# Moving a block's input scaling, its cast, a query cast and the output scaling to GpSimd, with a new order of steps

## The chip, the cores and the metric

The kernel runs on one core of one Trainium2 chip. The metric is the device time of the whole kernel in microseconds, as the median of several runs. Four engines compute: TensorE (PE in the profile, its weight loads PEld), VectorE (DVE), ScalarE (ACT) and GpSimd (POOL); SyncE (SP) issues most DMAs. Each engine takes its instructions strictly in program order and waits on semaphores for the others.

## The reference

An attention over pooled keys is followed by two feed-forward layers of 128 x 2048 x 128, all on 12288 rows of 128 columns:

```python
def _attn_ref(q, kv, w_sr):                # kv is pooled 4 x 4 to 768 keys; k = v = pooled @ w_sr
    s = scale * (q @ k.transpose(0, 2, 1))
    s = s - s.max(-1, keepdims=True)
    a = np.exp(s)
    a /= a.sum(-1, keepdims=True) + 1e-09
    return (a @ v).astype(np.float32)

def _moe_ref(x, w_in, w_out):              # layer 1
    h = x @ w_in
    relu6 = np.clip(h + 3.0, 0.0, 6.0)
    g = h * relu6 / 6.0
    return (g @ w_out).astype(np.float32)

def _moe2_ref(x, w_in, w_out):             # layer 2, beta = 1
    h = x @ w_in
    g = np.where(h >= beta, h, np.where(h <= -beta, 0.0, (h + beta) ** 2 / (4.0 * beta)))
    return (g @ w_out).astype(np.float32)
```

## The kernel before

The rows are cut into 24 blocks of 512, the 2048 hidden columns into 8 pairs of two chunks of 128. One block and one pair make a slot's work for a layer: slot T works on pair T of layer 1 (192 pairs in all) and on pair T - 11 of layer 2. Nearly every operand is kept as two fp16 parts, a high part (a cast) and a low part (what the cast lost), and each product is three matmuls: high x high, low x high, high x low. So a slot has 12 matmuls into the hidden activations (line 707, tiles `h`, a ring of four buffers in PSUM) and 12 into the two accumulators (line 725, `acc`), all of 512 columns. In a block of eight slots, four slots (even ones) also have the six score matmuls of 128 queries (line 593), and two (1 and 5 mod 8) the 18 matmuls that multiply weights by values (line 673).

The order of all steps is written out by hand: a prologue, then for slots below 22 the string RAMP, from slot 22 on the string SLOT. A name followed by `:n` serves slot T - n when slot T is issued. Every step issues to fixed engines, so a string is at once the order of five queues. The names, with the line of their main instruction and 0 and 1 for the two chunks:

- Layer 1: `a` matmuls (707, TensorE), `r` rectifier (749, ScalarE), `m` product (756, VectorE), `c` cast to the high part (785, ScalarE), `l` low part (791, GpSimd), `o` output matmuls (725).
- Layer 2: `A` matmuls (707), `K` clip (764, VectorE), `Q` square (772, ScalarE), `X` maximum (777, VectorE, it frees the `h` buffer), `C` cast (785, ScalarE), `L` low part (791, GpSimd), `O` output matmuls (725).
- Between the layers, once per block: `D` maximum of layer 1's output (490, VectorE), `R` copy of it to `xr` (496, ScalarE), `P` its sum over partitions (499, TensorE), `F` the scale and five columns of constants made from it (506 to 511, VectorE), `G` the high part x2h (516, ScalarE), `H` the low part x2l (521, VectorE). With `:1` and `:2` these fall in slots 1 and 2 mod 8; layer 2 reads x2 from slot 3 mod 8 on.
- Output, once per block: `T` transpose of the accumulator (734, VectorE), `U` scaling (739, ScalarE) and four DMAs (741, SyncE), in slot 5 mod 8.
- Queries, once per block: `q` transpose (558, VectorE) and a load, `i` high part (565, ScalarE), `j` low part (571, GpSimd); `q` and `i` in slot 2 mod 8.
- Attention: `s` scores, `n` their maximum (604, VectorE), `e` exponential (633, ScalarE), `t` sum and reciprocal (642, 645, VectorE), `u` high part of the weights (652, ScalarE), `w` low part (657, VectorE) and a transposing DMA (663), `v` values (673), `z` and `y` the two parts of layer 1's input (681 ScalarE, 687 VectorE).
- `B0` to `B2` convert weights; they are over by slot 22, and so is `x`.

Of the kernel before, what the change touches and what calls it, by code (L numbers as in the profile page):

```python
# [15 lines left out]
ACTF = mybir.ActivationFunctionType  # L16
ALU = mybir.AluOpType
# [20 lines left out]
RAMP = """a0:0 r0:0 a1:0 r1:0 t:1 u:1 m0:0 m1:0 D:1 R:1 G:2 H:2 x:0 A0:0 K0:0 A1:0 K1:0 C0:1 L0:1 C1:1 L1:1 c0:0 l0:0 c1:0 l1:0  # L38
T:3 U:3 Q0:0 Q1:0 s:0 n:0 w:1 P:1 F:1 X0:0 X1:0 e:0 v:0 z:0 y:0 q:0 i:0 j:0 B1:1 B2:2 B0:0 f o:1 O:2"""
SLOT = """  # L40
a0 r0 B2:3 o:2 a1 l1:1 u:1 O:3 G:2 r1 y:1 D:1 B0:2 C0:1 R:1 m0 A0 A1 v w:1 c0 H:2 C1:1 j:1 m1 c1 K0
K1 Q0 P:1 T:3 L0:1 s n q F:1 Q1 B1:3 L1:1 X0 e X1 f:1 t U:3 i z l0
"""
MX = ((0, "m8"), (1, "m10 m12"), (2, "m14 a2 b2"), (3, "s2 m9"), (4, "m11 m13"), (5, "m15 a3 b3"), (6, "s3 bk"))

# [14 lines left out]
def tile_attn_moe_moe2(  # L60
# [15 lines left out]
    nc = tc.nc  # L76
# [7 lines left out]
    KC = NKEY // 128  # L84
    scale = 1.0 / float(C) ** 0.5
# [32 lines left out]
    b_k = const.tile([128, 5], FP32, name="b_k")  # L118
# [12 lines left out]
    def new_h():  # L131
        return ps_h.tile([128, 512], FP32, tag="h", name="h")


    did = set()

    def step(name, key, *before):
        for n in before:
            assert (n, key) in did, (name, key, n)
        did.add((name, key))  # L140
# [27 lines left out]
    def died(rec):  # L168
        clock[0] += 1
        rec["dead"] = clock[0]  # L170
# [25 lines left out]
    def w_max(job):  # L196
        m, which, i = job
        n = 2 * m + (which == "out")
        nc.vector.tensor_reduce(out=mw[n][:, i:i + 1], in_=wst[job][0][:, :, 1].bitcast(FP32),
                                axis=AX.X, op=ALU.max, apply_absolute_value=True)  # L200

    def w_top(n):
        nc.vector.tensor_reduce(out=mw[n][:, 0:1], in_=mw[n], axis=AX.X, op=ALU.max)

    def w_top_pool(n):
# [2 lines left out]
        w_tops[n] = mw[n][:, 1:2]  # L210

    def w_top_row(n):
        step("row", n)
        w_tops[n] = new_h()
        nc.tensor.transpose(w_tops[n][0:1, 0:128], mw[n][:, 0:1], ident)

# [151 lines left out]
    def pool_ps(m):  # L368
        if m not in ps_pool:
            ps_pool[m] = new_h()  # L370
        return ps_pool[m]

    def kv_pool(i):
        m, mode = i // 2, KV_MODE[i]
        t = kv_t[i][0]
        if mode == "V":
            nc.vector.tensor_tensor(out=t[:, :, 0:2], in0=t[:, :, 0:2], in1=t[:, :, 2:4], op=ALU.add)
            nc.vector.tensor_tensor(out=t[:, :, 0], in0=t[:, :, 0], in1=t[:, :, 1], op=ALU.add)
            return
        ps = pool_ps(m)  # L380
        for g in range(2):
            p0 = (2 * (i % 2) + g) * 32
            for j in range(4):
                if mode == "P":
                    nc.tensor.matmul(ps[p0:p0 + 32, :128], pool_m, t[:, g, j], start=(j == 0), stop=(j == 3))
                else:
                    nc.tensor.matmul(
                        ps[:, 128 + p0:160 + p0], t[:, g, j], pool_m, start=(j == 0), stop=(j == 3)
                    )
        died(kv_t[i][1])  # L390
        if mode == "P" and i % 2 == 1:
            nc.scalar.copy(out=pk[:, m * 128:(m + 1) * 128], in_=ps[:, :128])

    def kv_sum_mm(i):
        t, rec = kv_t[i]
        ps = pool_ps(i // 2)
        for g in range(2):
            c0 = 128 + (2 * (i % 2) + g) * 32
            nc.tensor.matmul(ps[:, c0:c0 + 32], t[:, g, 0], pool_m)
        died(rec)  # L400
# [20 lines left out]

    def v_max(m):
        vp = vps[m // 3][:, (m % 3) * 128:(m % 3 + 1) * 128]
        nc.vector.tensor_reduce(
            out=mx[:, m:m + 1], in_=vp, axis=AX.X, op=ALU.max, apply_absolute_value=True
        )

    def v_scale():
        nc.vector.tensor_reduce(out=mx[:, 0:1], in_=mx, axis=AX.X, op=ALU.max)
        nc.tensor.transpose(vps[0][0:1, 384:512], mx[:, 0:1], ident)  # L430

# [54 lines left out]
    bs_t, mb_t, xr_t, x2_ps = {}, {}, {}, {}  # L486
# [15 lines left out]
    def x2_scales(b):  # L502
        step("F", b, "P")
        assert ("bk", 0) in did
        t = bs_t[b]
        nc.vector.tensor_scalar(out=t[:, 2:3], in0=x2_ps.pop(b)[:, 0:1], scalar1=2.0 ** -40, scalar2=None, op0=ALU.max)  # L506
        nc.vector.tensor_scalar(out=t.bitcast(U32)[:, 3:4], in0=t.bitcast(U32)[:, 2:3], scalar1=0x7F800000,
                                scalar2=None, op0=ALU.bitwise_and)
        nc.vector.reciprocal(out=t[:, 4:5], in_=t[:, 3:4])
        nc.vector.tensor_scalar(out=t[:, 5:8], in0=b_k[:, 0:3], scalar1=t[:, 4:5], scalar2=None, op0=ALU.mult)  # L510
        nc.vector.tensor_scalar(out=t[:, 8:10], in0=b_k[:, 3:5], scalar1=t[:, 3:4], scalar2=None, op0=ALU.mult)  # L511

    def x2_hi(b):
        step("G", b, "F")
        x2_t[b] = [x_p.tile([128, BLK], FP16, tag=f"x2{p}", name=f"x2{p}") for p in "hl"]
        nc.scalar.activation(out=x2_t[b][0], in_=xr_t[b], func=ACTF.Copy, scale=bs_t[b][:, 5:6])

    def x2_lo(b):
        step("H", b, "G")
        hi, lo = x2_t[b]  # L520
        nc.vector.scalar_tensor_tensor(  # L521
            out=lo, in0=xr_t.pop(b), scalar=bs_t[b][:, 5:6], in1=hi, op0=ALU.mult, op1=ALU.subtract
        )

    def v_hi(sv):
        for h in range(2):
# [15 lines left out]
    q_t, qT_t, e_t, at_t, x_t, x2_t, o_t = {}, {}, {}, {}, {}, {}, {}  # L542
# [19 lines left out]

    def q_hi(b):
        hi, lo, t = qT_t[b]
        nc.scalar.copy(out=hi, in_=t)
        step("i", b)

    def q_lo(b):
# [167 lines left out]

    def o_scale(b):
        o = o_t.pop(b)
        nc.scalar.activation(out=o, in_=o, func=ACTF.Copy, scale=bs_t[b][:, 9:10])
        for a in range(4):  # L740
            nc.sync.dma_start(
                out=o_v[b, a], in_=o[32 * a:32 * a + 32].rearrange("i (b j) -> i b j", j=32)
            )
# [51 lines left out]
    def ok(s):  # L795
        return 0 <= s < NS

    steps_m1 = {f"m{n}": (lambda n=n: w_max(w_jobs[n])) for n in range(8, 16)}
    for n in (2, 3):
        steps_m1 |= {f"a{n}": lambda n=n: (w_top(n), w_top_row(n)), f"b{n}": lambda n=n: w_top_all(n),  # L800
                     f"s{n}": lambda n=n: w_scale8(n)}
# [97 lines left out]
    with tc.manual_schedule():  # L899
# [6 lines left out]
            out=pool_m.rearrange("p (a q) -> p a q", a=4),  # L906
            in_=ident.rearrange("p (a r q) -> p a q r", a=4, r=4), axis=AX.X, op=ALU.add,
# [16 lines left out]
        for n, v in enumerate((2.0 ** -5, 2.0 ** -2, 2.0 ** -30)):  # L924
            nc.vector.memset(w_k[:, n:n + 1], v)

        steps = {f"k{i}": (lambda i=i: kv_pool(i)) for i in range(NG // 2)}
        steps |= {f"g{i}": (lambda i=i: kv_sum_mm(i)) for i in range(NG // 2)}
        for m in range(KC):
# [7 lines left out]
        for n in range(8):  # L937
            steps[f"m{n}"] = lambda n=n: w_max(w_jobs[n])
        steps |= {"ia": lambda: (w_top(0), w_top_pool(0)), "ib": lambda: (w_scales(0), w_unit(0)),
                  "oa": lambda: w_top(1), "ot": lambda: w_top_row(1), "ob": lambda: w_top_all(1),  # L940
                  "oc": lambda: w_scale8(1)}
        for j in range(4):
# [47 lines left out]
```

## Time and profile before

| What | Value |
|---|---|
| runs | 1339.81, 1341.2, 1343.64 us; median 1341.2 |
| profiled execution | 1342.52 us, its span 1340.7 us |
| TensorE busy | 1247.0 us, 93% |
| VectorE busy | 1187.5 us, 89% |
| ScalarE busy | 1158.6 us, 86% |
| GpSimd busy | 941.9 us, 70% |
| mean granted TensorE clock | 0.978 of full speed |

The profile shows one execution. Its span runs from the first to the last instruction, and 1.8 us of the execution's time lie outside. Times in rows are microseconds from the span's start; `L521` is line 521 of the kernel; `x2` at the end of a row counts merged instructions; what stands in square brackets is the engine's idle time before the row, with what ended it. A wait for several semaphores is put down to the one that came last. The ends of matmuls are modelled, so their starts are the better guide.

### The profile page before, as it was taken

The numbers are of one execution on the slowest core, as the hardware profiler recorded it, in microseconds if no ns is written. First come the engines' busy times: TensorE is split into PE (matmuls) and PEld (weight loads), VectorE is DVE, ScalarE is ACT, GpSimd is POOL, SyncE is SP. The second block draws the span as 40 slices with busy tenths as digits, with TensorE's granted clock in tenths as the row PEclk, the third lists the DMA queues.
The fourth block names the chain that finished last, engine by engine and source line by source line (L and its number), as shares of the span: only waits on it lengthen the run. The fifth ranks groups of instructions, "written<-read, shape, count | busy, mean of one in ns | idle before, by whom it ended". The sixth has DMA issues, their size and how long they took to land.

```text
span 1340.7 us, 19138 instructions
## 1 busy us (share of the span) xinstructions
PE 1247.0 (93%) x6280; PEld 662.2 (49%) x6280; DVE 1187.5 (89%) x1944; ACT 1158.6 (86%) x2028; POOL 941.9 (70%) x825
## 2 busy tenths in 40 slices
PE   7466789999999999999999999999999999999996
PEld 6333445455455555555455555555555555555442
DVE  4676799999999999999999999999999999999887
ACT  3465788998999998999998998899999999999986
POOL 2244687777777777777777777777777777777874
PEclk9687899999999999999999999999999999999998
DMA  8821113222222212222122122222122121121000
GB/s 301 219 44 36 32 26 50 44 39 45 39 37 53 40 35 52 36 40 52 32 44 52 33 44 49 33 46 47 36 45 44 37 48 36 32 45 32 1 9 17
DMA packets 260788, 66.32 MB, mean 49 GB/s; under 512 B 252368, under 2 KB 256592, under 8 KB 260688
## 3 DMA queue, kind: packets, MB, share of 16 engines
q1 hardware_dynamic: 257888, 63.73, 23.8%
q10 hardware_dynamic: 2800, 1.38, 0.4%
q8 instruction: 49, 0.80, 0.2%
q14 instruction: 51, 0.42, 0.1%
HBM read 21.04 MB, written 6.29 MB: 20 GB/s over the span
## 4 chain that ended last, share of the span: by engine, by line
PE 59%; DVE 20%; ACT 11%; issue 1%; DVEq 0%; ACTq 0%
PE h L707 24%; PE acc L725 23%; PE s L673 6%; PE s L593 5%; DVE g L777 5%; ACT h L785 4%; DVE g L764 3%; ACT t L749 2%; DVE t L756 2%; DVE x2l L521 2%; DVE bs L511 2%; ACT g L772 2%; ACT a L652 2%; DVE nm L604 2%; DVE bs L510 1%
## 5 line engine op out<-in xcount | busy, mean ns | idle before, releaser
L791 POOL TENSOR_TENSOR l<-g,h 128x512 f16<-128x512 f32 x382 | 450.1, 1196 | 274.7 <-DVE a L657 135.0
L791 POOL TENSOR_TENSOR l<-t,h 128x512 f16<-128x512 f32 x382 | 438.6, 1170 | 42.2 <-ACT h L785 39.2
L764 DVE TENSOR_SCALAR g<-h,bs 128x512 f32<-128x512 f32 x384 | 292.7, 804 | 23.7 <-PE h L707 23.6
L756 DVE SCALAR_TENSOR_TENSOR t<-t,h 128x512 f32<-128x512 f32 x384 | 255.8, 682 | 29.1 <-ACT t L749 25.9
L777 DVE SCALAR_TENSOR_TENSOR g<-g,bs,h 128x512 f32<-128x512 f32 x384 | 267.9, 737 | 14.0 <-ACT g L772 13.2
L785 ACT CAST h<-g 128x512 f16<-128x512 f32 x384 | 235.1, 615 | 42.2 <-PE acc L725 40.2
L749 ACT ACTIVATE t<-h,h_sc 128x512 f32<-128x512 f32 x384 | 252.5, 676 | 21.1 <-PE h L707 21.0
L772 ACT ACTIVATE g<-g,bs 128x512 f32<-128x512 f32 x384 | 259.7, 717 | 6.8 <-DVE g L764 3.6
L785 ACT CAST h<-t 128x512 f16<-128x512 f32 x384 | 235.6, 618 | 22.6 <-DVE t L756 21.2
L707 PE MATMUL h<-x2h,wi1h 128*128 128x512 f16 x384 | 145.6, 379 | 16.8 <-DVE g L777 16.8
L707 PE MATMUL h<-xh,wi0h 128*128 128x512 f16 x384 | 146.8, 382 | 10.2 <-ACT xh L681 6.2
L725 PE MATMUL acc<-h,wo1h 128*128 128x512 f16 x384 | 146.0, 380 | 3.9 <-DVE o L734 3.8
L725 PE MATMUL acc<-l,wo1h 128*128 128x512 f16 x384 | 145.9, 380 | 1.5 <-POOL l L791 1.5
L725 PE MATMUL acc<-h,wo0h 128*128 128x512 f16 x384 | 146.5, 381 | 0.8 <-DVE bs L506 0.8
L725 PE MATMUL acc<-l,wo0h 128*128 128x512 f16 x384 | 146.3, 381 | 0.5 <-DVE l L791 0.5
L725 PE MATMUL acc<-h,wo0l 128*128 128x512 f16 x384 | 146.1, 380 | 0.0
L725 PE MATMUL acc<-h,wo1l 128*128 128x512 f16 x384 | 146.0, 380 | 0.0
L707 PE MATMUL h<-xl,wi0h 128*128 128x512 f16 x384 | 145.9, 380 | 0.1
L707 PE MATMUL h<-xh,wi0l 128*128 128x512 f16 x384 | 146.0, 380 | 0.0
L707 PE MATMUL h<-x2h,wi1l 128*128 128x512 f16 x384 | 145.7, 379 | 0.0
L707 PE MATMUL h<-x2l,wi1h 128*128 128x512 f16 x384 | 145.5, 379 | 0.0
L707 PEld LDWEIGHTS <-wi1h 128*128 128x128 f16 x768 | 75.1, 98 | 113.9 <-issue 26.9
(183 smaller groups left out, 1843.6 us busy)
## 6 DMA issues: line engine op xcount, KB each, us to landing
out_dram<-o SPq DMA_DIRECT2D x96, 64.0 KB, 1.9
q<-in_q_dram SPq DMA_DIRECT2D x92, 64.0 KB, 2.3
wst<-in_kv_dram SPq DMA_DIRECT2D x9, 512.0 KB, 7.5
wst<-in_moe_w_in_dram SPq DMA_DIRECT2D x6, 512.0 KB, 6.2
wst<-in_moe_w_out_dram SPq DMA_DIRECT2D x5, 512.0 KB, 4.8
at<-a SPq DMA_TRANSPOSE x96, 3.7
g<-in_moe_w_out_dram SPq DMA_DIRECT2D x2, 512.0 KB, 7.9
g<-in_moe_w_in_dram SPq DMA_DIRECT2D x1, 512.0 KB, 4.2
```

Of the source, the lines that this page charges most:

```text
L511: nc.vector.tensor_scalar(out=t[:, 8:10], in0=b_k[:, 3:5], scalar1=t[:, 3:4], scalar2=None, op0=ALU.mult)
L593: nc.tensor.matmul(ps[h], l[:, js], r[:, ks], start=(n == 0), stop=(n == 2))
L673: nc.tensor.matmul(ps, l[:, k, :], r[:, k, :], start=(n == 0), stop=(n == 3 * KC - 1))
L707: nc.tensor.matmul(ps, l[:, ws], r, start=(n == 0), stop=(n == 2))
L725: nc.tensor.matmul(acc[m], l[:, ws], r[:, k, :], start=(c == 0 and i == 0), stop=(c == NPAIR - 1 and i == 5))
L749: nc.scalar.activation(out=g_t[0, s][:, k], in_=h_t[0, s, k], func=ACTF.Relu, scale=h_sc, bias=0.5 * H_SC)
L756: nc.vector.scalar_tensor_tensor(out=g, in0=g, scalar=H_SC, in1=h_t.pop((0, s, k)), op0=ALU.min, op1=ALU.mult)
L764: nc.vector.tensor_scalar(out=g_t[1, s][:, k], in0=h_t[1, s, k], scalar1=bs_t[s // NPAIR][:, 6:7], scalar2=bs_t[s // NPAIR][:, 7:8], op0=A ...
L772: nc.scalar.activation(out=g, in_=g, func=ACTF.Square, scale=bs_t[s // NPAIR][:, 8:9], bias=0.5)
L777: nc.vector.scalar_tensor_tensor(out=g, in0=g, scalar=bs_t[s // NPAIR][:, 6:7], in1=h_t.pop((1, s, k)), op0=ALU.mult, op1=ALU.max)
L785: nc.scalar.copy(out=hl_t[m, s][0][:, k], in_=g_t[m, s][:, k])
L791: eng.tensor_tensor(out=lo[:, k], in0=g_t[m, s][:, k], in1=hi[:, k], op=ALU.subtract)
```

## The change

Five things change, and nothing else that issues an instruction:

- The two products that make the five columns of constants (510, 511) leave `F` on VectorE and become the first two instructions of `G` on GpSimd.
- `G` now scales `xr` in place on GpSimd, and `H` makes the high part by a cast and the low part by a subtraction, both on GpSimd. Before, ScalarE made the high part by a scaled copy, and VectorE the low part in one instruction that scaled and subtracted.
- `U` scales the output on GpSimd in place of ScalarE.
- `i` casts the queries on GpSimd in place of ScalarE, for blocks from 2 on.
- SLOT has a new order. RAMP stays, so in slots below 22 the moved steps keep their places.

```diff
 SLOT = """
-a0 r0 B2:3 o:2 a1 l1:1 u:1 O:3 G:2 r1 y:1 D:1 B0:2 C0:1 R:1 m0 A0 A1 v w:1 c0 H:2 C1:1 j:1 m1 c1 K0
-K1 Q0 P:1 T:3 L0:1 s n q F:1 Q1 B1:3 L1:1 X0 e X1 f:1 t U:3 i z l0
+a0 L1:2 X1:1 t:1 r0 u:1 l0:1 o:2 z:1 a1 D:1 O:3 r1 A0 A1 q l1:1 G:2 y:1 v m0 w:1 C0:1 m1 R:1 T:3 i
+C1:1 c0 K0 K1 P:1 f:1 s j:1 U:3 c1 Q0 n B0:2 Q1 F:1 L0:1 H:2 B2:2 X0 B1:4 e
 """
...
         nc.vector.reciprocal(out=t[:, 4:5], in_=t[:, 3:4])
-        nc.vector.tensor_scalar(out=t[:, 5:8], in0=b_k[:, 0:3], scalar1=t[:, 4:5], scalar2=None, op0=ALU.mult)
-        nc.vector.tensor_scalar(out=t[:, 8:10], in0=b_k[:, 3:5], scalar1=t[:, 3:4], scalar2=None, op0=ALU.mult)
 
     def x2_hi(b):
         step("G", b, "F")
+        t, xr = bs_t[b], xr_t[b]
         x2_t[b] = [x_p.tile([128, BLK], FP16, tag=f"x2{p}", name=f"x2{p}") for p in "hl"]
-        nc.scalar.activation(out=x2_t[b][0], in_=xr_t[b], func=ACTF.Copy, scale=bs_t[b][:, 5:6])
+        nc.gpsimd.tensor_scalar(out=t[:, 5:8], in0=b_k[:, 0:3], scalar1=t[:, 4:5], scalar2=None, op0=ALU.mult)
+        nc.gpsimd.tensor_scalar(out=t[:, 8:10], in0=b_k[:, 3:5], scalar1=t[:, 3:4], scalar2=None, op0=ALU.mult)
+        nc.gpsimd.tensor_scalar(out=xr, in0=xr, scalar1=t[:, 5:6], scalar2=None, op0=ALU.mult)
 
     def x2_lo(b):
         step("H", b, "G")
         hi, lo = x2_t[b]
-        nc.vector.scalar_tensor_tensor(
-            out=lo, in0=xr_t.pop(b), scalar=bs_t[b][:, 5:6], in1=hi, op0=ALU.mult, op1=ALU.subtract
-        )
+        xr = xr_t.pop(b)
+        nc.gpsimd.tensor_copy(out=hi, in_=xr)
+        nc.gpsimd.tensor_tensor(out=lo, in0=xr, in1=hi, op=ALU.subtract)
...
     def q_hi(b):
         hi, lo, t = qT_t[b]
-        nc.scalar.copy(out=hi, in_=t)
+        (nc.gpsimd.tensor_copy if b > 1 else nc.scalar.copy)(out=hi, in_=t)
         step("i", b)
...
     def o_scale(b):
         o = o_t.pop(b)
-        nc.scalar.activation(out=o, in_=o, func=ACTF.Copy, scale=bs_t[b][:, 9:10])
+        nc.gpsimd.tensor_scalar(out=o, in0=o, scalar1=bs_t[b][:, 9:10], scalar2=None, op0=ALU.mult)
```

The rest of the diff adds assertions on the order of steps, which issue nothing.

## Rows read from the trace of the kernel before

**Rows 1.** The chain that ended last, in time: start us, us, what.

```profile
248.69 1.97 PE s L673 x18
...
704.71 1.97 PE s L673 x18
...
755.83 1.97 PE s L673 x18
...
805.94 1.97 PE s L673 x18
...
1160.72 1.97 PE s L673 x18
```

**Rows 2.** The same chain, six matmuls of 512 columns and six of scores.

```profile
798.39 1.29 PE h L707 x6
799.68 1.06 PE s L593 x6
```

**Rows 3.** Timeline, line 521 and GpSimd in two neighbouring blocks: start, us, engine, line.

```profile
711.37 1.73 DVE L521 SCALAR_TENSOR_TENSOR x2l<-xr,bs,x2h 128x512 f16<-128x512 f32 x1
711.38 2.73 POOL L791 TENSOR_TENSOR l<-g,h 128x512 f16<-128x512 f32 x2 [2.20 <-ACT h L785]
...
762.47 0.74 DVE L521 SCALAR_TENSOR_TENSOR x2l<-xr,bs,x2h 128x512 f16<-128x512 f32 x1
762.50 2.86 POOL L791 TENSOR_TENSOR l<-g,h 128x512 f16<-128x512 f32 x2 [2.21 <-ACT h L785]
```

**Rows 4.** Four lines alone: ns minimum/median/maximum, first and last start us.

```profile
L510 DVE TENSOR_SCALAR bs<-b_k,bs x24: 478/764/942, 139.9 to 1299.7; 128x3 f32<-128x3 f32 x24
L511 DVE TENSOR_SCALAR bs<-b_k,bs x24: 215/1198/1203, 140.7 to 1300.1; 128x2 f32<-128x2 f32 x24
L521 DVE SCALAR_TENSOR_TENSOR x2l<-xr,bs,x2h x24: 736/744/1733, 148.1 to 1301.5; 128x512 f16<-128x512 f32 x24
L657 DVE SCALAR_TENSOR_TENSOR a<-e,rc,a x96: 999/1018/1839, 46.3 to 1223.8; 128x768 f16<-128x768 f32 x96
```

**Rows 5.** Timeline of slots 106 to 108, four engines.

```profile
758.02 2.27 POOL L791 TENSOR_TENSOR l<-t,h 128x512 f16<-128x512 f32 x2
...
761.74 0.62 ACT L785 CAST h<-g 128x512 f16<-128x512 f32 x1 [0.61 <-PE acc L725]
...
765.17 0.94 DVE L604 TENSOR_REDUCE nm<-s 128x1 f32<-128x768 f32 x1
...
766.66 1.36 DVE L777 SCALAR_TENSOR_TENSOR g<-g,bs,h 128x512 f32<-128x512 f32 x2
...
767.79 0.38 PE L707 MATMUL h<-x2h,wi1h 128*128 128x512 f16 x1
...
772.60 1.41 DVE L777 SCALAR_TENSOR_TENSOR g<-g,bs,h 128x512 f32<-128x512 f32 x2 [0.21 <-ACT g L772]
...
773.40 0.38 PE L707 MATMUL h<-x2h,wi1h 128*128 128x512 f16 x1 [0.27 <-DVE g L777]
```

**Rows 6.** Groups on GpSimd: xcount, busy us, mean ns of one, idle us before.

```profile
L791 POOL TENSOR_TENSOR l<-t,h 128x512 f16<-128x512 f32 x382 | 438.6, 1170 | 42.2 <-ACT h L785 39.2 <-DVE bs L507 3.0
L571 POOL TENSOR_TENSOR ql<-qT,qh 128x512 fp32r<-128x512 f32 x24 | 30.6, 1273 | 36.8 <-ACT qh L565 35.6
...
L333 POOL CAST wo1h<-wst 128x512 f16<-128x512 f32 x4 | 2.6, 649 | 0.0
```

**Rows 7.** Timeline, TensorE at the start of slot 12.

```profile
154.34 0.38 PE L707 MATMUL h<-xh,wi0h 128*128 128x512 f16 x1 [2.71 <-DVE t L756]
```

**Rows 8.** Timeline of the tail, VectorE and TensorE.

```profile
1311.12 1.52 DVE L764 TENSOR_SCALAR g<-h,bs 128x512 f32<-128x512 f32 x2
1312.56 0.71 DVE L734 STREAM_TRANSPOSE o<-acc 128x512 f32<-128x512 f32 x1
...
1313.32 0.61 PE L725 MATMUL acc<-h,wo1h 128*128 128x512 f16 x1 [3.79 <-DVE o L734]
1313.72 0.63 PE L725 MATMUL acc<-l,wo1h 128*128 128x512 f16 x1
```

More of the change, by code (lines that the diff above doesn't have):

```diff
@@ L198, in w_max @@
         n = 2 * m + (which == "out")
+        step("max", (n, i))
         nc.vector.tensor_reduce(out=mw[n][:, i:i + 1], in_=wst[job][0][:, :, 1].bitcast(FP32),
@@ L204, in w_top @@
     def w_top(n):
+        step("top", n)
+        for i in range(4):
+            assert ("max", (n, i)) in did
         nc.vector.tensor_reduce(out=mw[n][:, 0:1], in_=mw[n], axis=AX.X, op=ALU.max)
@@ L212, in w_top_row @@
     def w_top_row(n):
-        step("row", n)
+        step("row", n, "top")
         w_tops[n] = new_h()
@@ L374, in kv_pool @@
         m, mode = i // 2, KV_MODE[i]
+        step("k", i)
         t = kv_t[i][0]
@@ L395, in kv_sum_mm @@
         t, rec = kv_t[i]
+        step("g", i, "k")
         ps = pool_ps(i // 2)
@@ L423, in v_max @@
         vp = vps[m // 3][:, (m % 3) * 128:(m % 3 + 1) * 128]
+        step("y", m)
         nc.vector.tensor_reduce(
@@ L428, in v_scale @@
     def v_scale():
+        for m in range(KC):
+            assert ("y", m) in did
         nc.vector.tensor_reduce(out=mx[:, 0:1], in_=mx, axis=AX.X, op=ALU.max)
```

## The prediction

> **What bounds the kernel now.** I read the page's engine table first: TensorE is busy 93% of the span, VectorE 89%, ScalarE 86%, GpSimd 70%. A busy TensorE proves little, because the ends of matmuls are modelled, so I went on to the chain that ended last. In it the 18 matmuls that multiply attention weights by values come back twice in each block of eight slots, and two such pieces, eight slots apart, give the length of a block [rows 1]. There are only two lengths: 755.83 - 704.71 = 51.12 us, a long block, and 805.94 - 755.83 = 50.11 us, a short one. From 248.69 to 1160.72 there are 18 blocks in 912.03 us: 18 x 50.11 = 901.98, and the other 10.05 us make 10 long blocks and 8 short ones. One more short block follows.
>
> What would a block take if TensorE never waited? Six matmuls of 512 columns take 1.29 us, a group of six score matmuls 1.06 [rows 2], 18 value matmuls 1.97 [rows 1]. A slot has four groups of the first kind, a block four score groups and two value groups: 32 x 1.29 + 4 x 1.06 + 2 x 1.97 = 49.5 us. With the rounding of 1.29 (one matmul is some 0.2155 us) and the switches between kinds I take 49.7. So a long block holds 1.4 us of waiting and a short one 0.4: 10 x 1.4 + 9 x 0.4 = 17.6 us. TensorE bounds the middle of the kernel, and this is all that any change to the other engines can win there.
>
> Where does a long block's extra 1.0 us come from? From one instruction: VectorE's line 521 (layer 2's low part) takes 1.73 us in a long block and 0.74 in a short one [rows 3]. In the long one GpSimd's subtraction starts within 0.01 us of it, in the short one 0.03 us after it. Lines 510 and 511, which multiply three and two columns, show the same: from 0.48 to 0.94 us and from 0.215 to 1.20 us for almost no data, medians 0.76 and 1.20 [rows 4]. These instructions touch nothing but on-chip memory, and stand still while a GpSimd instruction runs. The delayed VectorE queue reaches TensorE through the ring of buffers for the hidden activations: even in the short block the first layer-2 matmul of slot 108, at 773.40, waits for line 777 of slot 107, which started at 772.60 [rows 5]. TensorE could have started it 24 matmuls after the same matmul of slot 107 (767.79): at 772.96. That is the short block's 0.4 us.
>
> **The change part by part.** I follow this short block, whose x2 is prepared in slot 106.
>
> *Removed from VectorE, per block:* lines 510 and 511, 0.76 + 1.20, and line 521, 0.74 or 1.73: 2.7 or 3.7 us [rows 3, 4]. *Removed from ScalarE:* the x2 cast, the output's scaling and, for blocks from 2 on, the query cast. None of TensorE's waits named above ends on these, so they get nothing by themselves.
>
> *Added to GpSimd, per block:* two column products, a 512-column product, two casts (x2, queries) and a subtraction, and the output's product three slots later. The trace has the subtraction at 1.17 and a cast at 0.65 us [rows 6]. A product with a per-partition factor it does not show on GpSimd: it lies between the cast's 0.65 and the 1.27 of the costliest two-input form [rows 6]; I take 0.7, near the cast, as both read one input. A column product lies between nothing and a cast of 512 columns, 0.65; I take 0.15, as it has almost no data. So the steps that prepare x2 cost 0.3 + 0.7 + 0.65 + 1.17 = 2.8 us, the query cast 0.65, the output 0.7: 4.2 us, on top of 32 x 1.17 + 1.27 = 38.7 in a block of 50. GpSimd stays below TensorE.
>
> *Does it fit in time?* All of it but the output falls into slot 106. GpSimd ends the layer-1 subtractions of slot 105 at 758.02 + 2.27 = 760.3 [rows 5]. G would end at 761.3, the query cast at 761.95. Layer 2's subtraction waits for ScalarE's cast, 761.74 + 0.62 = 762.4 [rows 5], and ends at 763.5. H (cast and subtraction) ends at 765.3. TensorE wants x2 at 767.79: 2.5 us to spare. Three subtractions on, the second layer-1 low part of slot 106 is done at 765.3 + 3 x 1.17 = 768.8; the output matmuls of slot 108 want it 13 matmuls after 767.79, at 770.6: 1.8 to spare. At the upper ends above (1.0 + 0.57 more) 0.2 is left.
>
> *What comes late next?* The VectorE queue. In slot 106 the score maximum starts at 765.17 [rows 5], though its scores are there some 1.1 us earlier, 18 matmuls before 767.79 plus 0.2. Without the three instructions it starts at 764.1, and the query transpose (moved ahead) no longer stands between it and line 777, which then starts at 765.1 in place of 766.66 [rows 5]. What hangs on it moves forward by as much, less the half microsecond by which ScalarE's c0 now waits for C1: line 777 of slot 107 starts at 772.60 - 1.55 + 0.5 = 771.55 and ends its first half at 772.3. TensorE wants that buffer at 772.96. So the short block's wait goes too, if nothing is held: 0.7 us are left.
>
> *What the move adds:* line 657 reads two on-chip tensors, and now meets a GpSimd without a pause in slot 107. It took 1.02 us at the median but 1.84 at most [rows 4]: it can be held, by up to the 1.17 of a subtraction, and line 777 then misses its time by 0.5 us. Between nothing and the present 0.4 I take 0.2 us of waiting in each of 19 blocks, 3.8 us. A rule speaks against the move here: the Trainium skill, SBUF — State Buffer, section "SBUF: two separate sides", says that VectorE instructions with two on-chip inputs and GpSimd instructions share one port pair, held for a whole instruction. By that rule line 657 would pay at each of its four places (rival A); the 1.73 against 0.74 agrees with it.
>
> *The new order* keeps TensorE's own order (a0, o, a1, O, A0, A1, v, P, s) and GpSimd's cycle of subtractions; l0 and L1 only slide over the slot's edge. On VectorE the query transpose moves ahead of the slot's products, where it fills time before the layer-2 matmuls, and T comes before K0, K1. Line 741's four output DMAs wait on SyncE's queue for GpSimd in place of ScalarE; the transposes of the weights queue behind them, but none is due for another slot. The assertions issue nothing.
>
> *Slots below 22 (old order):* block 0's line 521 (148.1) [rows 4] stands in a VectorE run for whose line 756 TensorE waits at slot 12 (154.34, 2.71 us) [rows 7]; I take its 0.7 us, between 0 and 2.5, the three instructions of this block.
>
> *The tail:* after the last layer-1 slot VectorE has K0, K1, X0, X1 and little else. Lines 510, 511 and 521 are 0.48 + 0.21 + 0.74 = 1.4 us of its own queue there. TensorE stands for 3.8 us until line 734 has emptied the accumulator at 1312.56; in VectorE's queue that line stands behind a pair of line 764 (1311.12, 1.52 us) [rows 8], and T is now in front of the pair. Together 1.4 + 1.4 = 2.8 us, between 0 and 4.3: after the pause seven matmuls start about 0.4 us apart in place of 0.22 [rows 8], at the lower of the two clock levels, and a shorter pause might spare these 1.5. The last output scaling changes its engine; at 0.65 to 1.27 on GpSimd I give it nothing, ±0.5.
>
> *Sum:* 17.6 - 3.8 + 0.7 + 2.8 = 17.3 us. From the profiled execution's 1342.5 that is 1325.2; this execution lies 1.3 above the median of the runs, so 1341.2 - 17.3 = 1323.9. That the three runs differ by almost 4 us fits blocks that turn out long or short one by one. At the bounds 17.6 + 2.5 + 4.3 = 24.4: 1316.8.
>
> **The rivals.** *A, the port keeps its price.* GpSimd is busy for 43 of 50 us, so line 657 is held, four times a block, and the queue behind it keeps the waits: the long blocks' extra goes (10 us), the short block's 0.4 grows by another 0.45, since not one but two slots miss their time, and the ramp and tail give 3.5: 10 - 19 x 0.45 + 3.5 = 5 us, so 1336; between 1330 and 1340. For it: GpSimd's full slot 107. Against: slots 108 and 109 are lengthened on TensorE by attention matmuls.
>
> *B, GpSimd becomes the bound of slots 106 to 108, and the kernel slower.* The added work of slot 106 is 3.5 us with 1.8 to spare, so it decides from 5.3 us on. If the product and both casts take the 1.27 of the query's low part, and a column 0.65, it is 1.3 + 3.8 + 1.2 = 6.3; with half a hold by line 657 (0.5) 6.8. That is 1.5 us in each of 19 blocks, 28.5, against 17.6 + 3.5: 7 us slower, 1349; between 1341 and 1358. For it: nothing shows that product on GpSimd. Against: the trace's casts take 0.65.
>
> *C, nothing comes of it:* TensorE waits as long for another buffer of the ring; 1341.
>
> **How the numbers follow.** The forecast, 1317 to 1330, has 0.57; A 0.20, B 0.14, C 0.09. The range 1316 to 1340 leaves out B and half of C. A measurement of this kernel can tell some 0.3%, 4 us, from no change. Faster by more: the forecast and nearly all of A, 0.75; within 4 us 0.11; slower 0.14.
>
> **What would show it.** Blocks of one length near 49.9 us in the chain; no VectorE instruction like lines 510, 511, 521; H ending some 2 us ahead of x2's first matmul; GpSimd's product near 0.7 us. Line 657 much above 1.02 us would be A; TensorE waiting for GpSimd at line 725, or for x2, B; long blocks as before, C. In the tail, T ahead of the pair of line 764. The forecast is wrong above all if the walk through slot 107 leaves out a wait of half a microsecond.

## The result, and the profile after

The changed kernel takes 1326.45 us (median of 4 runs, 1324.85 to 1328.11) where the kernel before takes 1340.51 (4 runs, 1337.05 to 1343.64): ratio 0.9896, 95% interval 0.9868 to 0.9924. The profiled execution took 1325.94 us, its span is 1324.2 of these.

The head of the page, with the table of engines (busy us, share of the span, instructions), and the start of its chain:

```profile
span 1324.2 us, 19015 instructions
PE 1243.0 (94%) x6280; PEld 663.1 (50%) x6280; DVE 1150.0 (87%) x1872; ACT 1119.4 (85%) x1958; POOL 1083.8 (82%) x991
...
PE 80%; DVE 5%; ACT 3%; issue 1%; POOL 1%; POOLq 0%; ACTq 0%; DVEq 0%
```

The same line on the page of before:

```profile
PE 59%; DVE 20%; ACT 11%; issue 1%; DVEq 0%; ACTq 0%
```

The table hardly tells what happened: TensorE is one point busier, GpSimd twelve. The chain does: VectorE and ScalarE are nearly gone from it. In the middle it consists of TensorE alone. The chain after, the pieces that answer to [rows 1] and the neighbours of the second (line numbers are 10 higher from here on: 673 is now 683, 707 is 717, 725 is 735, 777 is 787, 791 is 801):

```profile
697.09 1.97 PE s L683 x18
...
746.77 1.97 PE s L683 x18
748.74 0.67 PE h L717 x3
749.41 1.29 PE acc L735 x6
...
796.45 1.96 PE s L683 x18
```

796.45 - 746.77 = 49.68 us, and 746.77 - 697.09 = 49.68 too. All 18 blocks between slots 32 and 176 have this length to within 0.01 us: 288.1 to 1182.3 is 894.2 us, where the kernel before took 288.2 to 1199.2, 911.0. There are no long and short blocks any more, and the view of TensorE's waits has no row between 290 and 1180 us. In the kernel before it has one there: line 707 waits 27 times for line 777, 9.2 us in all.

What the moved steps cost, GpSimd's lines (ns minimum/median/maximum, first and last start us) and VectorE's line 667, the 657 of [rows 4]:

```profile
L524 POOL TENSOR_SCALAR bs<-b_k,bs x24: 299/310/322, 146.9 to 1283.3; 128x3 f32<-128x3 f32 x24
...
L526 POOL TENSOR_SCALAR xr<-xr,bs x24: 1559/1568/1580, 147.5 to 1283.8; 128x512 f32<-128x512 f32 x24
L532 POOL CAST x2h<-xr x24: 599/612/632, 149.1 to 1286.5; 128x512 f16<-128x512 f32 x24
L533 POOL TENSOR_TENSOR x2l<-xr,x2h x24: 1153/1158/1162, 149.8 to 1287.1; 128x512 f16<-128x512 f32 x24
...
L749 POOL TENSOR_SCALAR o<-o,bs x24: 1562/1567/1571, 231.2 to 1317.7; 128x512 f32<-128x512 f32 x24
...
L667 DVE SCALAR_TENSOR_TENSOR a<-e,rc,a x96: 998/1094/2047, 45.9 to 1205.7; 128x768 f16<-128x768 f32 x96
```

The casts and the subtraction cost what the trace of before showed. The product with a per-partition factor costs 1.57 us: more than the 1.27 that I had given as its upper end, and more than the subtraction, which reads two inputs.

The timeline of slots 106 and 107, which answers to [rows 5]:

```profile
750.58 0.70 DVE L568 STREAM_TRANSPOSE qT<-q 128x512 f32<-128x512 f32 x1
...
755.04 0.96 DVE L614 TENSOR_REDUCE nm<-s 128x1 f32<-128x768 f32 x1
755.91 1.40 DVE L787 SCALAR_TENSOR_TENSOR g<-g,bs,h 128x512 f32<-128x512 f32 x2
...
758.62 2.02 DVE L667 SCALAR_TENSOR_TENSOR a<-e,rc,a 128x768 f16<-128x768 f32 x1 [0.30 <-ACT a L662]
...
762.75 1.47 DVE L787 SCALAR_TENSOR_TENSOR g<-g,bs,h 128x512 f32<-128x512 f32 x2
```

```profile
751.43 1.57 POOL L526 TENSOR_SCALAR xr<-xr,bs 128x512 f32<-128x512 f32 x1
...
755.32 1.16 POOL L533 TENSOR_TENSOR x2l<-xr,x2h 128x512 f16<-128x512 f32 x1
...
757.55 2.27 POOL L801 TENSOR_TENSOR l<-t,h 128x512 f16<-128x512 f32 x2
759.79 1.99 POOL L581 TENSOR_TENSOR ql<-qT,qh 128x512 fp32r<-128x512 f32 x1
```

```profile
758.74 0.38 PE L717 MATMUL h<-x2h,wi1h 128*128 128x512 f16 x1
...
763.91 0.38 PE L717 MATMUL h<-x2h,wi1h 128*128 128x512 f16 x1
```

The score maximum (line 614) starts 758.74 - 755.04 = 3.70 us ahead of slot 107's first layer-2 matmul; the prediction had 767.79 - 764.1 = 3.7. H ends at 756.48, 2.26 us ahead of it (predicted 2.5). The attention product, line 667, takes 2.02 us, where 1.02 was the median before: it is held for 1.0 us. All the same, the first half of line 787 of slot 107 is done at 762.75 + 0.73 = 763.48, and TensorE takes up that buffer at 763.91 without waiting.

The tail, GpSimd, VectorE and TensorE, which answers to [rows 8]:

```profile
1287.15 1.15 POOL L533 TENSOR_TENSOR x2l<-xr,x2h 128x512 f16<-128x512 f32 x1
...
1296.22 1.57 POOL L749 TENSOR_SCALAR o<-o,bs 128x512 f32<-128x512 f32 x1 [1.35 <-DVE o L744]
...
1317.71 1.56 POOL L749 TENSOR_SCALAR o<-o,bs 128x512 f32<-128x512 f32 x1 [3.30 <-DVE o L744]
```

```profile
1295.42 0.71 DVE L744 STREAM_TRANSPOSE o<-acc 128x512 f32<-128x512 f32 x1
1296.05 1.49 DVE L774 TENSOR_SCALAR g<-h,bs 128x512 f32<-128x512 f32 x2
...
1300.07 1.53 DVE L774 TENSOR_SCALAR g<-h,bs 128x512 f32<-128x512 f32 x2 [1.00 <-POOL l L801]
```

```profile
1288.36 0.38 PE L717 MATMUL h<-x2l,wi1h 128*128 128x512 f16 x1 [0.86 <-POOL x2l L533]
...
1296.18 0.39 PE L735 MATMUL acc<-h,wo1h 128*128 128x512 f16 x1 [1.41 <-ACT h L795]
```

Line 744 (T) now stands in front of the pair of line 774, and the pause of 3.79 us has shrunk to 1.41. But three GpSimd instructions have taken its place: the low part of x2 is 0.86 us late, the output's product holds up the subtractions (VectorE waits 1.00 us for one), and the last output's product takes 1.56 us at the very end. In the kernel before the granted clock had fallen to 0.51 of full speed from 1313 to 1316 us, behind the long pause; here it stays at 1.00 from 1296 to 1320.

Where the time went, by the start of the first matmul of slots 3, 22 and 191:

| stretch | before | after | measured change | predicted change |
|---|---|---|---|---|
| start to slot 3 | 88.0 | 91.0 | +3.0 | 0 |
| slots 3 to 22 | 140.3 | 138.5 | -1.8 | -0.7 |
| slots 22 to 191 | 1055.4 | 1037.3 | -18.1 | -13.8 |
| slot 191 to the end | 57.0 | 57.4 | +0.4 | -2.8 |
| span | 1340.7 | 1324.2 | -16.5 | -17.3 |

### The profile page after: what moved, and what is told of

The parts are those of the page before. It is cut to its first block, busy times and chain, and to the rows that moved or that the text cites. A ratio compares the mean times of both kernels' runs of the same rounds, so it can differ in the third digit from the quotient of the medians.

```text
span 1324.2 us, 19015 instructions
## 1 busy us (share of the span) xinstructions
PE 1243.0 (94%) x6280; PEld 663.1 (50%) x6280; DVE 1150.0 (87%) x1872; ACT 1119.4 (85%) x1958; POOL 1083.8 (82%) x991
## 4 chain that ended last, share of the span: by engine, by line
PE 80%; DVE 5%; ACT 3%; issue 1%; POOL 1%; POOLq 0%; ACTq 0%; DVEq 0%
PE acc L735 34%; PE h L717 34%; PE s L603 6%; PE s L683 6%; DVE g L787 1%; DVE g L774 1%; ACT h L795 1%; DVE t L766 1%; ACT g L782 1%; POOL l L801 1%; ACT t L759 0%; DVE nm L614 0%; ACT wr L284 0%; DVE wst L292 0%; PE h L683 0%
## 5 line engine op out<-in xcount | busy, mean ns | idle before, releaser
L801 POOL TENSOR_TENSOR l<-g,h 128x512 f16<-128x512 f32 x382 | 441.5, 1175 | 89.6 <-DVE a L667 59.1
L787 DVE SCALAR_TENSOR_TENSOR g<-g,bs,h 128x512 f32<-128x512 f32 x384 | 271.7, 742 | 14.7 <-ACT g L782 11.3
L795 ACT CAST h<-g 128x512 f16<-128x512 f32 x384 | 220.6, 615 | 42.4 <-PE acc L735 40.2
L795 ACT CAST h<-t 128x512 f16<-128x512 f32 x384 | 220.9, 617 | 17.2 <-DVE t L766 17.2
L667 DVE SCALAR_TENSOR_TENSOR a<-e,rc,a 128x768 f16<-128x768 f32 x96 | 125.9, 1312 | 21.7 <-ACT a L662 21.5
```

Of the source, the lines that this page charges most:

```text
L667: nc.vector.scalar_tensor_tensor(out=a[:, 1], in0=e, scalar=rc, in1=a[:, 0], op0=ALU.mult, op1=ALU.subtract)
L787: nc.vector.scalar_tensor_tensor(out=g, in0=g, scalar=bs_t[s // NPAIR][:, 6:7], in1=h_t.pop((1, s, k)), op0=ALU.mult, op1=ALU.max)
L795: nc.scalar.copy(out=hl_t[m, s][0][:, k], in_=g_t[m, s][:, k])
L801: eng.tensor_tensor(out=lo[:, k], in0=g_t[m, s][:, k], in1=hi[:, k], op=ALU.subtract)
```

## The experiments

The kernel before was timed beside each group of runs on one chip, and its time differs between chips: 1340.5 us above, 1351.45 (1341.88 to 1355.63) beside the first group, 1351.43 (1346.97 to 1358.16) beside the second, 1341.1 (1335.77 to 1345.49) beside the third. The changed kernel gives 1326.45 on the first chip and 1326.91 on the second group's. So ratios are compared inside a group only, and block lengths from the traces across groups.

### Group 1: the order, the move, and how much room GpSimd has

**The new order alone,** on the kernel before:

```diff
-SLOT = """ a0 r0 B2:3 o:2 a1 l1:1 u:1 O:3 G:2 r1 y:1 D:1 ...
+SLOT = """ a0 L1:2 X1:1 t:1 r0 u:1 l0:1 o:2 z:1 a1 D:1 O:3 ...
```

> The kernel before with the new order of slots from 22 on, every step on its old engine. If the gain comes from taking lines 510, 511 and 521 off VectorE, they are still there: the query transpose has moved out of the way (0.7 us), so the short blocks' 0.4 us may go, the long blocks stay, and the time is 1330 to 1342 us against 1340.5. If the order alone makes the gain, blocks of 49.7 us and 1322 to 1328.

Measured: 1328.61 us (1326.76 to 1331.08), ratio 0.9822 (0.9788 to 0.9856). Its timeline in the slot that prepares x2:

```profile
753.14 0.42 DVE L510 TENSOR_SCALAR bs<-b_k,bs 128x3 f32<-128x3 f32 x1
753.47 1.20 DVE L511 TENSOR_SCALAR bs<-b_k,bs 128x2 f32<-128x2 f32 x1
...
755.90 0.70 DVE L558 STREAM_TRANSPOSE qT<-q 128x512 f32<-128x512 f32 x1
...
760.33 0.83 DVE L521 SCALAR_TENSOR_TENSOR x2l<-xr,bs,x2h 128x512 f16<-128x512 f32 x1
```

Lines 510 and 511 are still on VectorE and line 511 is still held, yet the blocks are 49.87 us long and all but one alike (the other 50.18): 897.9 us from slot 32 to slot 176. The theory that the gain needs the three instructions to leave VectorE falls here.

How the order does it shows where the two timelines part. From line 506 to the pair of line 777 behind the score maximum VectorE works through the same instructions in both kernels with hardly a pause, only in another order. What differs is how long two of them are held. Line 510 ends when a subtraction of GpSimd ends. Before, that subtraction starts 0.42 us ahead of line 510, as GpSimd has just waited for a cast:

```profile
756.90 1.16 POOL L791 TENSOR_TENSOR l<-g,h 128x512 f16<-128x512 f32 x1 [0.31 <-ACT h L785]
758.44 0.76 DVE L510 TENSOR_SCALAR bs<-b_k,bs 128x3 f32<-128x3 f32 x1
```

With the new order GpSimd does not wait there, and it starts 0.76 us ahead:

```profile
752.38 2.27 POOL L791 TENSOR_TENSOR l<-t,h 128x512 f16<-128x512 f32 x2
```

So line 510 takes 0.42 us in place of 0.76. Line 521 now starts some 0.24 us ahead of a subtraction, no longer together with one, and takes 0.83 us in nearly every block: that ends the long blocks. Against a short block 0.34 - 0.09 = 0.25 us is gained, and the block is 50.11 - 49.87 = 0.24 us shorter. The 0.19 us that are left over the changed kernel's 49.68 stand at the first layer-2 matmul of slot 108 as before: it starts 0.40 us after the matmul ahead of it, where undisturbed ones are 0.22 apart.

**The move alone,** on the changed kernel with the old order:

```diff
-SLOT = """ a0 L1:2 X1:1 t:1 r0 u:1 l0:1 o:2 z:1 a1 D:1 O:3 ...
+SLOT = """ a0 r0 B2:3 o:2 a1 l1:1 u:1 O:3 G:2 r1 y:1 D:1 ...
```

> The changed kernel with the old order of slots: the moved steps are on GpSimd, nothing else differs. If taking the three instructions off VectorE makes the gain, no long blocks, at most the old short block's 0.4 us of waiting in each (19 x 0.4 = 8 us): 1326 to 1335. If the order is what is needed to make the move fit, H ends late or line 777's successor is delayed in each block: 1340 or more.

Measured: 1330.76 us (1329.24 to 1333.56), ratio 0.984 (0.9811 to 0.9869); 897.6 us from slot 32 to slot 176, all blocks 49.87. Against the first profile each half of the change does four fifths of the middle alone (13.1 and 13.4 us of 16.8), and they don't add up. But nine of these 18 blocks were long, and either half does away with that. Against short blocks of 50.11 us each takes off 0.24 us and both together 0.43. In the tail they pull in opposite directions: from slot 191 to the end it is 57.0 us before, 54.8 with the order alone, 58.9 with the move alone.

**One and two more products on GpSimd.** Into the step that scales x2, for blocks 2 to 22, go one or two further products of the same size, into a spare tile that nobody reads; the computation is otherwise whole.

```diff
+        if b > 1 and b < NB - 1:
+            nc.gpsimd.tensor_scalar(out=spare, in0=xr, scalar1=t[:, 5:6], scalar2=None, op0=ALU.mult)
```

> The changed kernel with one more 512-column product on GpSimd at the end of G, into a spare tile, for 21 of the 24 blocks: 1.57 us more in slot 2 mod 8. By the walk through the queues, H has 2.2 us to spare and the second layer-1 low part 1.7: nearly all is covered, 0 to 0.4 us a block, 1326 to 1335. If GpSimd's load is already passed on, the whole 1.57 x 21 = 33 us: 1359.

> The same with two more products, 3.14 us more in slot 2 mod 8. By the walk both margins are passed: H comes 0.9 us late for x2's first matmul and the second layer-1 low part 1.4 late, so some 1.4 us in each of 21 blocks, 29 us over the changed kernel: 1350 to 1360. If only GpSimd's mean load counts (43.8 + 3.1 = 47 of 50 us), nothing: 1326.

Measured: 1343.43 us (1340.27 to 1345.45), ratio 0.9933 (0.9908 to 0.9958), with one; 1378.04 us (1376.83 to 1379.17), ratio 1.0187 (1.0159 to 1.0215), with two. TensorE's waits between 290 and 1180 us (us in total, times, longest), of the first and of the second:

```profile
PE acc L738 <- POOL l L804: 5.6, 18, 0.3
```

```profile
PE acc L739 <- POOL l L805: 19.6, 34, 0.9
PE h L721 <- POOL x2l L537: 12.7, 17, 0.8
```

TensorE waits for GpSimd in these and for nothing else. (The view counts from the modelled end of the matmul before, so its sums are smaller than what the blocks lose.) A block takes 50.40 and 52.05 us in place of 49.68: 0.72 more for 1.57 us of added work, 2.37 for 3.14. What is left over is 1.57 - 0.72 = 0.85 and 3.14 - 2.37 = 0.77 us. So the changed kernel has some 0.8 us of room on GpSimd in a block, less than I expected, and beyond that each microsecond there costs one in every block. The page's 82% for GpSimd shows nothing of this edge.

### Group 2: the two ends

**The changed kernel again,** as the measure for this group.

> The changed kernel once more, on the chip of the next three, as their yardstick: 1326, and blocks of 49.7 us without waits. If the 3.0 us that it lost between slots 2 and 3 (a stretch at half the granted clock) is chance of the clock and not the change, slot 3 starts at 88 to 91 us from run to run.

Measured: 1326.91 us (1325.36 to 1328.17). Blocks of 49.68 us, 57.2 us from slot 191 to the end.

**The tail given back:** x2 of the last block and the last two outputs on the engines they had before.

```diff
-        nc.gpsimd.tensor_scalar(out=xr, in0=xr, scalar1=t[:, 5:6], scalar2=None, op0=ALU.mult)
+        if b == NB - 1:
+            nc.scalar.activation(out=x2_t[b][0], in_=xr, func=ACTF.Copy, scale=t[:, 5:6])
...
+        if b >= NB - 2:
+            nc.scalar.activation(out=o, in_=o, func=ACTF.Copy, scale=bs_t[b][:, 9:10])
```

> The changed kernel, but the last block's x2 and the last two blocks' output scaling are on the old engines. If the tail lost its forecast gain because GpSimd's product takes 1.57 us (2.4 us and 1.0 us of VectorE waiting, 0.85 at the very end) and VectorE takes back 1.4 of its own, this is 2 to 4 us faster than the changed kernel. If the tail is bound by VectorE's own sequence anyway, 0 to 1 us.

Measured: 1324.55 us (1322.68 to 1325.8), 2.4 less than the changed kernel beside it; the tail is 54.6 us, 2.6 shorter, and the middle the same.

**Outputs and query casts back on ScalarE,** in all blocks; only x2 stays on GpSimd:

```diff
-        nc.gpsimd.tensor_scalar(out=o, in0=o, scalar1=bs_t[b][:, 9:10], scalar2=None, op0=ALU.mult)
+        nc.scalar.activation(out=o, in_=o, func=ACTF.Copy, scale=bs_t[b][:, 9:10])
...
-        (nc.gpsimd.tensor_copy if b > 1 else nc.scalar.copy)(out=hi, in_=t)
+        nc.scalar.copy(out=hi, in_=t)
```

> The changed kernel, but the output scaling and all query casts are back on ScalarE; only the x2 steps stay on GpSimd, in the new order. If the middle needs nothing of the other two, its blocks stay at 49.7 us, and the tail gains 1 to 2.5 us (the output product of 1.57 us no longer stands in front of the low parts and the end): 1 to 2.5 us faster. If ScalarE's relief matters in the middle, 0.2 us or more a block slower, 3 us in all.

Measured: 1324.65 us (1323.04 to 1327.69). The middle stays at 49.68 us a block, the tail is 55.3. So of the moved steps the output's and the query's give nothing in the middle, and the output's product costs 57.2 - 55.3 = 1.9 us in the tail. The medians differ by 2.3 us, but the spreads overlap; the tail's lengths carry the statement.

**The query casts of blocks up to 4 on ScalarE,** to see whether the 3 us at slots 2 to 3 come from them:

```diff
-        (nc.gpsimd.tensor_copy if b > 1 else nc.scalar.copy)(out=hi, in_=t)
+        (nc.gpsimd.tensor_copy if b > 4 else nc.scalar.copy)(out=hi, in_=t)
```

> The changed kernel, but the query casts of blocks 2 to 4 (slots below 22) stay on ScalarE. If the 3 us lost between slots 2 and 3 come from the clock, no difference, within 1.5 us of the changed kernel. If the cast on GpSimd delays the early slots, 2 to 4 us faster.

Measured: 1327.87 us (1324.75 to 1328.1): no difference. Slot 3 starts at 91.8 us, in the changed kernel beside it at 92.2. So the cast is not their cause. The time goes with the granted clock: windows of the changed kernel's first profile (from:to, length, TensorE busy, granted clock, DMA share, GB/s):

```profile
82.00:86.00 4.00, 1.33 (x6) 0.86 0.52 98
86.00:90.00 4.00, 4.00 (x12) 0.50 0.00 0
90.00:94.00 4.00, 4.00 (x17) 0.78 0.59 110
```

From 86 to 90 us TensorE ran 12 matmuls at 0.50, the lower of the two levels (1.2 GHz), after 1.33 busy us in the four before. The kernel before ran 21 at 1.00 there, after the same 1.33 busy us:

```profile
86.00:90.00 4.00, 4.00 (x21) 1.00 0.00 0
```

From the start of slot 2 to that of slot 3 it takes 7.2 us at 1.00, the changed kernel 9.9 us at a mean of 0.67, in both of its profiles. The kernel with the move alone, which issues the same steps below slot 22 as the changed one, takes 7.2 at 1.00: the moved steps are not the cause. Slot 3 starts anywhere between 88.0 and 93.3 us in the profiles of this study, in those of the kernel before (88.0 and 91.7) as in those of the changed one (91.0 and 92.2), and part of this spread arises ahead of slot 2; what sets the clock there wasn't found.

### Group 3: what makes the blocks long or short

**The kernel before once more.**

> The kernel before, unchanged, once more, to count its long blocks (51.1 us) and short ones (50.1 us) in another execution. If a long block comes from a race of some 10 to 30 ns between line 521 and GpSimd's subtraction, the mixture of the first execution (10 long, 9 short) is no property of the kernel: another execution may have anything from 0 to 19 long ones, and its time should then be 1332 us plus 1 us for each long one; a time of 1351 us goes with 19. If something else makes the executions differ, the count stays near 10 and the difference stands elsewhere.

Measured: 1341.13 us (1336.3 to 1342.47), ratio 0.9996 (0.9977 to 1.0015); the profiled execution 1339.17. Its chain, line 521 (ns minimum/median/maximum) and the two instructions that meet, on VectorE and on GpSimd:

```profile
705.53 1.96 PE s L673 x18
...
755.65 1.97 PE s L673 x18
...
805.76 1.97 PE s L673 x18
```

```profile
L521 DVE SCALAR_TENSOR_TENSOR x2l<-xr,bs,x2h x24: 735/740/1680, 151.8 to 1297.4; 128x512 f16<-128x512 f32 x24
```

```profile
762.30 0.74 DVE L521 SCALAR_TENSOR_TENSOR x2l<-xr,bs,x2h 128x512 f16<-128x512 f32 x1
```

```profile
762.32 2.86 POOL L791 TENSOR_TENSOR l<-g,h 128x512 f16<-128x512 f32 x2 [2.21 <-ACT h L785]
```

Not one of the 18 blocks from slot 32 on is long: 50.11 us each, 902.1 in all, where the first profile has nine long ones. (The block ahead of them, the first of the 19 that the prediction counts, is long in both.) VectorE comes 0.02 us ahead of GpSimd here, as in the short blocks of [rows 3], and GpSimd is the one that stands still: the first of its two subtractions takes 1.74 us in place of 1.16. Read to the nanosecond, line 521 starts 21 ns or more ahead of the subtraction in each short block of the two profiles, and 18 ns or less ahead, or behind it, in each long one. So nine of the 10 long blocks of the first profile belong to that execution, not to the kernel. The time by itself fell outside the expectation, since this execution lost 3.6 us before slot 3, 1.2 in slots 3 to 22 and 0.8 in the tail, of the 8.9 that it gained.

**Only H (line 521) later,** in front of X0, on the kernel before:

```diff
-... m0 A0 A1 v w:1 c0 H:2 C1:1 j:1 m1 c1 K0 ... B1:3 L1:1 X0 e ...
+... m0 A0 A1 v w:1 c0 C1:1 j:1 m1 c1 K0 ... B1:3 L1:1 H:2 X0 e ...
```

> The kernel before with one step moved in the written order, from slot 22 on: H (line 521) from behind c0 to in front of X0, as the new order has it; all engines as before. If the long blocks come from where line 521 stands, and not from its engine, they are gone: blocks of 50.1 us or less, 1328 to 1333 us. If the whole new order is needed (the query transpose ahead of the products, c0 behind C1), long blocks stay: 1340 to 1351 us.

Measured: 1337.45 us (1333.55 to 1338.36), ratio 0.9967 (0.995 to 0.9984). The 18 blocks are 50.11 to 50.13 us, line 521 takes 0.70. No block is long. But line 521 still starts only 0.02 to 0.04 us ahead of a subtraction in all blocks but one, and the kernel before has an execution with the same short blocks, so this run doesn't show that its place makes them short. It makes them no shorter: VectorE has the same work ahead of line 777, and TensorE still waits for that. The expected 1328 to 1333 was too low, since I took off the long blocks from an execution whose slot 3 started at 88.0; here it starts at 93.1.

**Only q (the query transpose) earlier,** ahead of the products, on the kernel before:

```diff
-... G:2 r1 y:1 D:1 B0:2 ... s n q F:1 Q1 ...
+... G:2 r1 D:1 q y:1 B0:2 ... s n F:1 Q1 ...
```

> The kernel before with one other step moved, from slot 22 on: q (the query transpose) to ahead of the slot's products, as the new order has it; H stays behind c0, all engines as before. If line 521's hold makes the long blocks, they stay (up to 1.0 us each), and the earlier line 777 takes off at most the 0.4 us of a short block: 1336 to 1347 us. If the gain of the order comes from the query transpose, the blocks come out at 49.9 us: 1328 us.

Measured: 1350.33 us (1348.96 to 1352.68), ratio 1.0076 (1.0058 to 1.0095): slower than either theory had it. VectorE's timeline, and the matmul that waits:

```profile
764.10 0.70 DVE L558 STREAM_TRANSPOSE qT<-q 128x512 f32<-128x512 f32 x1
...
765.04 0.67 DVE L756 SCALAR_TENSOR_TENSOR t<-t,h 128x512 f32<-128x512 f32 x1
765.63 1.14 DVE L521 SCALAR_TENSOR_TENSOR x2l<-xr,bs,x2h 128x512 f16<-128x512 f32 x1
766.69 0.68 DVE L756 SCALAR_TENSOR_TENSOR t<-t,h 128x512 f32<-128x512 f32 x1
```

```profile
772.57 0.38 PE L707 MATMUL h<-xh,wi0h 128*128 128x512 f16 x1 [0.72 <-DVE t L756]
```

The transpose doesn't fill idle time there; with line 521 still between the two halves of line 756 it pushes them and what follows them back, and line 521 takes 1.14 us there. TensorE then waits 0.72 us for layer 1's line 756, and the blocks are 50.87 us (one 51.17). So neither step of the order does it alone. H later without q earlier gives 50.11, q earlier without H later 50.87, and the whole order 49.87. The two without the rest of the order were not run; the rest also moves the casts and subtractions on which the hold of line 510 hangs (group 1).

**Only x2 on GpSimd, in all blocks but the last,** on the changed kernel:

```diff
-        nc.gpsimd.tensor_scalar(out=o, in0=o, scalar1=bs_t[b][:, 9:10], scalar2=None, op0=ALU.mult)
+        nc.scalar.activation(out=o, in_=o, func=ACTF.Copy, scale=bs_t[b][:, 9:10])
...
+        if b == NB - 1:
+            nc.scalar.activation(out=x2_t[b][0], in_=xr, func=ACTF.Copy, scale=t[:, 5:6])
```

> The changed kernel with only layer 2's x2 on GpSimd, in all blocks but the last: the output's scaling and the query cast on ScalarE, and the last block's x2 on the engines before. If the losses of the tail are the product of 1.57 us in the last blocks and the subtraction that waits on GpSimd, it lies below each of the two kernels that give back one of them (1324.6 there): 1321 to 1324 us, with the middle's blocks at 49.7 us. If the two repair the same wait, 1324.5 us.

Measured: 1324.77 us (1321.72 to 1325.49), ratio 0.9875 (0.9859 to 0.9892). Blocks of 49.68 us, tail 54.7: 0.6 less than with x2 of the last block on GpSimd. So the output's product is most of the tail's loss and x2 the rest. (The expected 1321 to 1324 split this badly: the last outputs were back on ScalarE in both of the kernels that it compares with.) Against the changed kernel's ratio of 0.9896 this is no difference that the intervals tell apart; the trace of the tail shows 2.6 us.

## Why the prediction was right, step by step

**The time.** 1323.9 was forecast, 1326.45 measured, inside the forecast's own 1317 to 1330. But the terms missed in ways that cancel (the table above): the middle gave 4.3 us more, slots 3 to 22 gave 1.1 more, the tail 3.2 less, and the first slots took 3.0 that no step foresaw. The number also leans on the execution that was profiled, with its ten long blocks: against the second profile of the kernel before, the middle gives 9.2 us in place of 18.1 and the span 13.2 in place of 16.5. So that it came so close to the sum is luck.

**TensorE as the bound, and the block's floor.** Right: 49.7 us from [rows 1, 2], 49.68 measured. The waiting of 1.4 us in a long block and 0.4 in a short one is confirmed by 51.12 and 50.11 against it.

**The leftover at line 657.** Mis-sized. I took 0.2 us of waiting a block, 3.8 in all, for a hold of up to 1.17. The hold came, 1.0 us in slot 107 and its like in each of the 19 blocks and 0.2 in slot 109, but the waiting was nothing. The walk through slot 107 had put line 787 only 0.7 us ahead of its time, with half a microsecond taken off for c0 behind C1. With the hold it is still 763.91 - 763.48 = 0.43 ahead, so without one it would be about 1.4, an estimate: that half microsecond was not paid, and 0.2 more was there. Line 787 starts within 0.1 us behind line 774, so ScalarE kept it waiting no longer than that.

**Rival A and the port.** The Trainium skill, SBUF — State Buffer, section "SBUF: two separate sides", has VectorE instructions with two on-chip inputs and GpSimd instructions share one port pair that is held for a whole instruction. The trace agrees in kind: 2.02 for 1.02 us on line 667, and 1.99 for 1.27 on GpSimd's query subtraction a microsecond later. But only two of the four attention products of a block are held (one by 1.0, one by 0.2 us), and neither reaches TensorE. A hold of up to 1.17 us was right; A's count and its way to TensorE were not.

**GpSimd's costs and rival B.** The product was mis-sized (0.7 taken, 1.27 at most, 1.57 measured) and so was a column product (0.15 taken, 0.30 measured); the casts and the subtraction were right. The added work of slot 106 is 0.31 + 0.30 + 1.57 + 0.61 + 0.61 + 1.16 = 4.56 us, not 3.5. The point from which B decides was forecast at 5.3, and the two loaded kernels put it at 4.56 + 0.8 = 5.4. The mechanism of B is thus shown to be there, 0.8 us away. The range for the product was too narrow because I took the costliest row of GpSimd as a ceiling for an operation of another kind.

**Rival C** is out: no buffer of the ring keeps TensorE waiting in the middle.

**What the new order does.** Here the working was wrong though the sum was not. I gave the middle to the three instructions that leave VectorE, and of the order I said that it keeps GpSimd's cycle and that "l0 and L1 only slide over the slot's edge", at no price. The order alone, with every step on its old engine, takes off the long blocks and 0.24 us of a short one: line 521 no longer starts together with a subtraction, and line 510 is held 0.34 us less. The sentence that q "fills time before the layer-2 matmuls" is true only once the three instructions are gone: with them VectorE has hardly a pause there. With the move alone line 787 of slot 106 starts 2.20 us ahead of slot 107's first layer-2 matmul, with the new order as well 2.83.

**Where the long blocks come from.** The mechanism was right (line 521 against GpSimd's subtraction), but the sum took 10 long and 9 short ones as given, though the prediction itself remarked that they might turn out one by one. It is a race of some 0.02 us, which one execution loses in nine of 18 blocks and another in none of the same 18. That the kernel before takes 1351 us on two other chips would fit blocks that are all long: 1342.5 + 9 more of 1.0 us = 1351.5. No trace of it was taken there, so this stays open.

**The ramp and the tail.** Slots 3 to 22 gave 1.8, within the 0 to 2.5 of the forecast: they take 138.5 to 139.2 us in every profile with x2 on GpSimd and 140.2 to 141.4 in every one without. In the tail T in front of the pair of line 764 did what was said of it (3.79 to 1.41, and the order alone takes 2.2 us off the tail). The shorter pause also spared the fall of the clock, which the forecast had named and left out of its sum. The 1.4 us from lines 510, 511 and 521 did not come: the order alone, which leaves them on VectorE, already has a tail of 54.8 us, and in the two that are shorter (54.6 and 54.7) the last block's are on VectorE as well. The other step that failed is "The last output scaling changes its engine; at 0.65 to 1.27 on GpSimd I give it nothing, ±0.5": it also stands in GpSimd's queue ahead of subtractions that VectorE waits for, and the 1.57 us ran out uncovered at the end. That is 1.9 us, and the last x2 another 0.6.

## What to carry to other kernels

When an instruction stands between two that feed the bound, look first whether its place is wrong before moving it to another engine: order and engine drew on the same holds here, and either alone took away the long blocks and over half of a short one's wait. Compare the durations of the same instructions before and after: line 510's 0.42 us in place of 0.76 told more than the order's text. Count long and short blocks in a second execution before giving their difference to a change. A busy share says little about room: GpSimd at 82% had 0.8 us left in a block of 49.7, and an added load of known size is the way to measure this. A step that is free in the steady middle is paid for in the tail, where nothing covers it; the last block may keep its old engine.

## What the runs showed of the hardware

- A 128x512 fp32 product with a per-partition factor takes 1.57 us on GpSimd, the two-input subtraction to fp16 1.16, a cast 0.61; products of three or two columns still take 0.31 and 0.30.
- When a VectorE and a GpSimd instruction with on-chip operands meet, either can stand still. In the steady blocks of the kernel before, line 521 takes 0.74 us where it starts 21 to 34 ns ahead of GpSimd's subtraction, which then takes 1.74 us in place of 1.16; it takes 1.67 to 1.73 us where it starts 18 ns or less ahead, or behind. The same block can go either way in two executions.
- A product of three columns on VectorE that meets a subtraction on GpSimd ends when that ends: it takes 0.76 us with the old order of steps and 0.42 with the new.
- From the start of slot 2 to that of slot 3 one execution of the kernel before took 7.2 us at a granted clock of 1.00 and another 8.5 at a mean of 0.86.
